# Another order for the second part of a hand-ordered attention and gated-convolution kernel

## The chip, the cores and the metric

The kernel runs on one core of one Trainium2 chip. The metric is the device time of one execution in microseconds (us). A core has TensorE (matmuls; PE in the profile, its weight loads PEld), VectorE (DVE), ScalarE (ACT), GpSimd (POOL) and SyncE (SP), which here issues most of the transfers. Each engine works through its own queue in order and waits where an operand or a buffer isn't ready.

## The reference

Two layers follow each other. The first is attention in which a query sees the first four keys (the sinks) and the 128 keys up to itself; the second takes its output `x`, gates a projection by a convolution of five taps, and projects again.

```
scores = scale * q @ k^T                    # 4 batches, 8 heads, 768 positions, 64 wide
keep   = (pos_k < 4) | (0 <= pos_q - pos_k < 128)
a      = softmax(where(keep, scores, -1e9))
x      = concat_heads(a @ v)                # 4 x 768 x 512
gate   = sigmoid(sum_k conv_w[k] * x shifted by 4 - k)
out    = (gate * (x @ w_val)) @ w_out
```

## The kernel before

`banded` (from L193) cuts the work into 24 steps s = 0 to 23: four batches, three parts of 256 positions (p = 0, 1, 2), and two halves of the heads. Two steps of one batch and part make a pair m = 0 to 11, for which the second layer runs. The order of the work isn't found by a scheduler. `ORDER` (L36 to L81) is a string of 849 names, and the last lines of `banded` call one small function for each name under `manual_schedule`, so that every engine takes its instructions in the order of that list:

```python
with tc.manual_schedule():
    for n in ORDER.split():
        f, args = events[n]
        f(*args)
```

The names, with the step or pair behind the point, and the engine that works:

- `kq`, `vv`: loads of keys and queries, and of values (three buffers each), issued by SyncE; where p = 0, `vv` also loads the sinks' values, and `sv` (ScalarE, then GpSimd) splits them.
- `s0`, `s1` (L395 to L411): scores of one half of the step, 64 TensorE matmuls that use the array in tiles of 64 by 32, then masking and the maximum on VectorE. `e0`, `e1` (L413): the exponentials on ScalarE. `rec`, `norm`: the reciprocal and the products on GpSimd.
- `tx` (L448): 16 transposes of the weights on TensorE, tiles of 64 by 128. `px` (VectorE) and `py` (ScalarE) copy them out. `sk` (L461): one transpose of the sinks' weights, full array; `ts` copies it out, on ScalarE for steps under 6 and on VectorE from there on.
- `vl` (L500): weights by values, 48 matmuls (32 where p = 0), tiles of 64 by 64, into the one buffer `xv`. `si` (L517): two matmuls more for the sinks, tiles of 64 by 128, which end the same sums.
- `xc`, `xh`, `hd` (ScalarE) read `xv`; `xl` (GpSimd) makes the low half of x; `c4` (GpSimd) and `c0`, `c1` (VectorE, eight operations) are the convolution; `c0` and `c1` read `xv` too. `th` is the gate (ScalarE).
- `v0` to `v3` (L567): x by `w_val`, twelve matmuls each, full array, the last four with the low half. `g0`, `g1` (VectorE), `h0`, `h1` (ScalarE), `l0`, `l1` (GpSimd): the gated product and its two halves gh and gl.
- `o0` to `o3` (L607): by `w_out`, six matmuls each, full array (twelve of half the width for the last block). `t0`, `t1` (ScalarE) copy the sums out, `d0`, `d1` (SyncE) send them.

The PSUM memory that TensorE writes is shared out by two small rotations: `pairs`, two buffers that serve `s0`, `s1`, `tx` and at the end `o`, and `homes`, two that serve `sk`, `v` and `o`. A buffer is taken again when its last reader is done (`e0` or `e1` for scores, `px` and `py` for `tx`, `ts` for `sk`, `g` for `v`, `t` for `o`). `tx` of a step waits for its `norm`, `vl` for `px` and `py` and for the convolution of the step before.

Of the kernel before, what the change touches and what calls it, by code (L numbers as in the profile page):

```python
# [51 lines left out]
h1.2 c1.6 e1.9 rec.9 l1.2 o3.2 e1.10 d1.0 t1.2 tx.8 xl.6 px.8 py.8 vl.7 si.7 xc.7 hd.7 xh.7 sk.8 norm.9 ts.8
c4.7 s0.10 tx.9 th.6 px.9 c0.7 d1.11 c1.7 o1.2 t0.2 e0.10 rec.10 xl.7 v0.3 vv.8 py.9 v1.3 vv.9 g0.3 h0.3 kq.12
s0.12 kq.11 s0.11 th.7 d1.2 l0.3 vl.8 si.8 xc.8 hd.8 c4.8 xh.8 d0.2 s1.11 sk.9 e0.11 norm.10 ts.9 xl.8 v2.3
e1.11 v3.3 c0.8 c1.8 g1.3 e0.12 h1.3 o2.3 s1.12 l1.3 kq.13 s1.13 rec.11 e1.12 rec.12 vl.9 si.9 xc.9 th.8 c4.9
hd.9 xh.9 tx.10 px.10 kq.16 py.10 o3.3 t1.3 vv.10 norm.11 o0.3 o1.3 t0.3 c0.9 c1.9 sk.10 ts.10 s0.13 tx.11
py.11 px.11 norm.12 xl.9 vv.13 vl.10 si.10 xc.10 hd.10 xh.10 kq.14 d1.3 tx.12 py.12 px.12 c4.10 c0.10 warm_up
v0.4 xl.10 v1.4 g0.4 d1.1 h0.4 l0.4 vv.11 c1.10 th.9 v2.4 e1.13 v3.4 g1.4 sk.11 ts.11 s1.14 s0.14 h1.4 vl.11
si.11 o0.4 sk.12 ts.12 e0.13 rec.13 l1.4 xc.11 hd.11 c4.11 sv.13 e0.14 norm.13 c0.11 o1.4 kq.18 e1.14 t0.4
c1.11 kq.15 o2.4 d0.3 o3.4 s0.18 s0.15 vv.12 th.11 xh.11 sv.12 vl.12 si.12 t1.4 xc.12 tx.13 rec.14 hd.12 xl.11  # L60
v0.5 c4.12 norm.14 xh.12 e0.15 px.13 c0.12 c1.12 v2.5 xl.12 v3.5 g1.5 py.13 th.10 v1.5 g0.5 h0.5 sk.13 ts.13
s1.15 h1.5 s1.18 d0.4 e1.15 vl.13 l0.5 si.13 o0.5 l1.5 xc.13 rec.15 hd.13 xh.13 s0.16 e0.16 th.12 tx.14 px.14
o2.5 kq.17 o1.5 t0.5 py.14 c4.13 c0.13 o3.5 t1.5 vv.14 e0.18 xl.13 vv.18 c1.13 s1.16 d1.5 sk.14 ts.14 norm.15
sk.15 ts.15 sv.18 vl.14 si.14 xc.14 hd.14 tx.15 px.15 e1.16 c4.14 c0.14 rec.16 py.15 norm.16 e1.18 c1.14 xh.14
v0.6 v1.6 g0.6 v2.6 h0.6 s0.17 vv.15 kq.19 s0.19 vl.15 si.15 rec.18 l0.6 th.13 vv.16 e0.17 xc.15 v3.6 g1.6
xl.14 c4.15 s1.17 hd.15 s1.19 th.14 h1.6 sk.16 ts.16 l1.6 xh.15 c0.15 xl.15 e1.17 rec.17 kq.20 e0.19 o0.6 o1.6
# [825 lines left out]
```

## Time and profile before

| | us |
|---|---|
| median of 3 runs | 263.9 |
| lowest and highest of the 3 | 263.66, 264.38 |
| the profiled execution's own time | 264.63 |
| its span, first to last instruction | 262.8 |
| TensorE busy | 253.6 |
| VectorE busy | 204.7 |
| ScalarE busy | 188.7 |
| GpSimd busy | 177.4 |

The profile is of one execution. Its engines' times are those in which an instruction was at work; the time of the execution holds the span and 1.8 us around it. Matmuls overlap, so the duration of one is longer than the distance to the next, and their ends are modelled; starts are recorded.

### The profile page before, as it was taken

Reading aid. Unit: us, or ns where it says so; the run is one execution under the profiler, and the core shown is the slowest. Engines: PE = TensorE matmul, PEld = TensorE weight load, DVE = VectorE, ACT = ScalarE, POOL = GpSimd, SP = SyncE. Lnnn points to the kernel's source line nnn. Section 1 sums busy time; section 2 is a strip of 40 time slices with the busy share of each in tenths; the row PEclk is TensorE's granted clock in tenths of the full one; section 3 lists DMA queues with packets and bytes.
Section 4 is the critical chain, followed back from the end, with each engine's and each line's share of the span. In section 5 each row is a group of like instructions: output and inputs, shape, how many; then the busy total and the mean of one; then the engine's idle time right before and its main releaser. Section 6 shows DMA issues by size and latency. Waiting matters only on the chain.

```text
span 262.8 us, 9921 instructions
## 1 busy us (share of the span) xinstructions
PE 253.6 (97%) x3960; PEld 205.5 (78%) x3964; DVE 204.7 (78%) x561; ACT 188.7 (72%) x692; POOL 177.4 (67%) x241
## 2 busy tenths in 40 slices
PE   7899989999999999999999999999999999999993
PEld 2355569779878878889879779889779788888982
DVE  5976999979979879997869698796878659667610
ACT  3899998979887677974796688986676768444231
POOL 6279897778668992878379665894782985933340
PEclk9999999999999999999999999999999999999998
DMA  6999382364323534755250529253407131030013
GB/s 201 379 340 341 113 262 74 109 168 144 106 78 118 183 131 146 218 171 180 63 174 2 161 81 326 78 185 111 142 4 231 68 106 59 2 122 0 2 44 128
DMA packets 27541, 36.45 MB, mean 139 GB/s; under 512 B 2272, under 2 KB 24032, under 8 KB 27488
## 3 DMA queue, kind: packets, MB, share of 16 engines
q1 hardware_dynamic: 26672, 34.96, 41.7%
q10 hardware_dynamic: 816, 0.79, 0.9%
q8 instruction: 33, 0.54, 0.9%
q14 instruction: 20, 0.16, 0.2%
HBM read 29.45 MB, written 6.29 MB: 136 GB/s over the span
## 4 chain that ended last, share of the span: by engine, by line
PE 79%; ACT 9%; POOL 4%; DMA 4%; DVE 1%; issue 1%; POOLq 0%
PE ac L576 24%; PE ac L629 22%; PE xv L513 11%; PE pr L395 9%; PE pr L455 4%; ACT w L420 4%; PE pr L629 3%; PE xv L521 2%; DMA raw<-in_w_val_dram 2%; DMA vs<-in_vsk_dram 2%; POOL xl L544 1%; PE ac L463 1%; POOL gl L605 1%; POOL vh L263 1%; ACT wv_p L140 1%
## 5 line engine op out<-in xcount | busy, mean ns | idle before, releaser
L557 DVE SCALAR_TENSOR_TENSOR sg<-xv,cw,sg 128x256 f32<-128x256 f32 x192 | 77.8, 474 | 3.3 <-POOL sg L549 2.9
L435 POOL TENSOR_TENSOR wx<-w,sm 128x512 f32<-128x512 f32 x48 | 49.2, 1047 | 5.7 <-DVE sm L427 4.0
L420 ACT ACTIVATE w<-pr,ngm 128x132 f32<-128x132 f32 x136 | 48.6, 370 | 1.6
L576 PE MATMUL ac<-xh,wvh 128*128 128x256 f32 x192 | 48.7, 288 | 0.0
L605 POOL TENSOR_TENSOR gl<-sg,gh 128x512 fp32r<-128x512 f32 x24 | 30.8, 1290 | 26.0 <-ACT gh L601 25.8
L576 PE MATMUL ac<-xh,wvl 128*128 128x256 f32 x192 | 47.0, 279 | 0.0
L549 POOL TENSOR_TENSOR sg<-xt,cw 128x512 f32<-128x512 f32 x24 | 25.5, 1063 | 17.9 <-ACT xt L528 16.5
L576 PEld LDWEIGHTS ac<-xh,wvh 128*128 128x128 f32 x192 | 36.2, 189 | 1.7 <-issue 0.5
L576 PEld LDWEIGHTS ac<-xh,wvl 128*128 128x128 f32 x192 | 36.1, 188 | 0.2
L395 PE MATMUL pr<-k,q 64*32 64x168 f32 x1536 | 35.0, 307 | 0.6 <-DVE wt L486 0.2
L513 PEld LDWEIGHTS xv<-wt,v 64*64 64x64 f32 x1024 | 30.3, 133 | 6.1 <-issue 2.6
L513 PE MATMUL xv<-wt,v 64*64 64x192 f32 (+2 forms) x1024 | 34.5, 278 | 0.2 <-ACT wt L494 0.2
L544 POOL TENSOR_TENSOR xl<-xt,xh 128x512 fp32r<-128x512 f32 x24 | 31.0, 1290 | 3.9 <-DVE sm L427 2.5
L629 PE MATMUL ac<-woh,gh 128*128 128x512 f32 x80 | 33.2, 415 | 0.0
L629 PE MATMUL ac<-woh,gl 128*128 128x512 f32 x80 | 31.8, 397 | 0.3 <-POOL gl L605 0.3
L629 PE MATMUL ac<-wol,gh 128*128 128x512 f32 x80 | 31.7, 396 | 0.0
L576 PE MATMUL ac<-xl,wvh 128*128 128x256 f32 x192 | 30.4, 280 | 0.1
L395 PEld LDWEIGHTS pr<-k,q 64*32 64x32 f32 x1536 | 24.0, 106 | 8.1 <-issue 2.1
L400 DVE COPY_PREDICATED pr<-low,pr 128x256 f32<-128x256 uint8 x48 | 20.3, 422 | 9.6 <-PE pr L395 4.9
L420 ACT ACTIVATION_READ_ACCUMULATOR w<-pr,ngm 128x1 f32 x136 | 27.6, 203 | 0.0
L576 PEld LDWEIGHTS ac<-xl,wvh 128*128 128x128 f32 x192 | 25.9, 188 | 0.3 <-POOL xl L544 0.3
L404 DVE TENSOR_REDUCE ngm<-pr 128x4 f32<-128x528 f32 x34 | 24.0, 707 | 1.2
(156 smaller groups left out, 480.0 us busy)
## 6 DMA issues: line engine op xcount, KB each, us to landing
k<-in_kt_dram SPq DMA_DIRECT2D x23, 408.0 KB, 4.1
v<-in_vt_dram SPq DMA_DIRECT2D x16, 384.0 KB, 3.9
q<-in_qt_dram SPq DMA_DIRECT2D x23, 256.0 KB, 4.6
out_dram<-osb SPq DMA_DIRECT2D x23, 256.0 KB, 2.5
v<-in_vt_dram SPq DMA_DIRECT2D x8, 256.0 KB, 5.0
raw<-in_w_out_dram SPq DMA_DIRECT2D x4, 512.0 KB, 6.6
raw<-in_w_val_dram SPq DMA_DIRECT2D x3, 512.0 KB, 6.3
raw<-in_w_val_dram ACTq DMA_DIRECT2D x1, 512.0 KB, 5.2
```

The source lines that it names most:

```text
L395: nc.tensor.matmul(ss[e * QB:(e + 1) * QB, j, c * n + x0:c * n + x1], q[js, g, (4 * c + e) * QB:(4 * c + e + 1) * QB], k[js, g, (2 * c + e ...
L400: nc.vector.copy_predicated(sv[:, :, :, :D], low[:, None, None, :].to_broadcast([P, 2, 2, D]), sv[:, :, :, 2 * HB:])
L404: nc.vector.tensor_reduce(out=ngm[:, g], in_=sv[:, :, :, :PK], axis=mybir.AxisListType.X, op=ALU.max)
L420: nc.scalar.activation(out=w[:, g, j, c], in_=sx[:, j, c, :PK], func=AF.Exp, scale=0.125 if whole else -1.0, bias=ngm[:, g, j, c:c + 1], a ...
L435: nc.gpsimd.tensor_tensor(out=t[:, n].rearrange("p c h x -> p h c x"), in0=w[:, :, :, at], in1=sm.to_broadcast([P, 4, 2, D]), op=ALU.mult)
L513: nc.tensor.matmul(acc[o * D:(o + 1) * D, g, x0 + h * D:x0 + (h + a1 - a0 + 1) * D], v[js, g, n], t[js, n % 2, n // 2, g, a0:a1 + 1].rearr ...
L544: nc.gpsimd.tensor_tensor(out=half(xls, s, "xl", F32R), in0=xts[s], in1=half(xhs, s, "xh", F32R).bitcast(F32), op=ALU.subtract)
L549: nc.gpsimd.tensor_tensor(out=half(sg, s, "sg", F32), in0=xts[s], op=ALU.mult, in1=cw[:, g, KT - 1:].to_broadcast([P, 2, PQ]))
L557: nc.vector.scalar_tensor_tensor(out=g, in0=x, scalar=a, in1=g, op0=ALU.mult, op1=ALU.add)
L576: nc.tensor.matmul(acc[:, h], a[:, kc, cs], x[:, kc], start=(n == 0), stop=(n == 11))
L605: nc.gpsimd.tensor_tensor(out=gl, in0=g, in1=gh.bitcast(F32), op=ALU.subtract)
L629: nc.tensor.matmul(acc, a[:, kc, ts], x[:, kc], start=(kc + n == 0), stop=(kc + n == 5))
```

## The change

The first 218 names of `ORDER` stay, which ends with `vv.4`, shortly ahead of the scores of step 7. The other 631 names are the same names in another order. Nothing else changes. Cut to the lines that the text speaks of:

```diff
@@ -45,39 +45,39 @@
-s0.7 l0.1 vl.4 y1.1 g1.1 e0.7 h1.1 l1.1 s1.7 s1.8 o2.1 si.4 e1.7 tx.5 xc.4 xh.4 px.5 hd.4 c4.4 c0.4 c1.4 o3.1
-t1.1 o0.1 e1.8 py.5 kq.9 sk.5 ts.5 norm.6 o1.1 t0.1 tx.6 py.6 rec.7 vl.5 si.5 xc.5 xl.4 px.6 c4.5 sk.6 ts.6
-hd.5 xh.5 xl.5 s0.9 s0.8 th.4 norm.7 v0.2 v1.2 e0.9 c0.5 tx.7 c1.5 e0.8 rec.8 norm.8 v2.2 py.7 px.7 g0.2 h0.2
...
-l1.7 vl.17 si.17 xc.17 c4.17 hd.17 xh.17 e0.21 xl.17 norm.20 d1.6 c0.17 tx.19 py.19 o2.7 o3.7 o1.7 t0.7 c1.17
-th.17 px.19 t1.7 kq.23 d1.7 s1.21 vl.18 d0.7 si.18 xc.18 c4.18 hd.18 vv.19 xh.18 e1.21 sv.19 tx.20 vv.20 px.20
...
-rec.21 s0.22 xc.19 hd.19 l0.8 xh.19 c4.19 xl.19 sk.20 o0.8 ts.20 o1.8 c0.19 c1.19 norm.21 e1.22 t0.8 d0.8 o2.8
...
-v2.10 v1.10 th.22 g0.10 v3.10 h0.10 l0.10 vl.23 si.23 xc.23 c4.23 hd.23 xh.23 xl.23 th.21 flag g1.10 o0.10
...
-o1.10 l1.11 o1.11 t0.10 d0.10 t0.11 o3.10 t1.10 o2.11 d1.10 d0.11 o3.11 t1.11
+y1.1 s1.7 s0.7 g1.1 vl.4 si.4 l0.1 tx.5 xc.4 xh.4 h1.1 c4.4 d1.0 hd.4 px.5 c0.4 c1.4 s1.8 vv.7 l1.1 sk.5 o2.1
+ts.5 norm.6 py.5 e0.7 e1.7 o0.1 o1.1 xl.4 rec.7 t0.1 vl.5 kq.10 tx.6 si.5 e1.8 py.6 xh.5 sk.6 warm_up norm.7
+o3.1 xc.5 ts.6 px.6 th.4 kq.9 xl.5 s0.8 t1.1 hd.5 e0.8 s0.9 c4.5 v0.2 c0.5 v1.2 sv.7 kq.12 g0.2 v2.2 rec.8
...
+ts.9 c0.8 c1.8 vv.9 v3.3 l0.3 d0.1 o2.3 g1.3 e0.11 e1.11 s1.13 th.8 norm.10 h1.3 xl.8 s0.13 rec.11 vl.9 l1.3
...
+c0.11 o1.4 vv.19 d0.3 c1.11 e1.14 norm.13 xh.11 tx.13 t1.4 d1.11 t0.4 px.13 xl.11 vl.12 si.12 s1.15 py.13
+xc.12 kq.19 hd.12 s0.15 v0.5 sv.13 th.10 th.11 xh.12 sk.13 c4.12 kq.16 vv.15 ts.13 rec.14 v1.5 c0.12 c1.12
...
+s0.16 sk.14 l1.5 xc.13 d0.4 c4.13 o0.5 xl.12 vv.14 ts.14 o1.5 c0.13 xl.13 e0.16 o2.5 c1.13 py.14 norm.15 s1.19
+s1.16 vl.14 tx.15 e1.18 t0.5 si.14 hd.14 xc.14 px.15 c4.14 o3.5 v0.6 t1.5 sk.15 e1.16 py.15 c0.14 ts.15 th.13
...
+tx.16 sk.16 v3.6 ts.16 hd.15 g1.6 py.16 xl.15 kq.20 v0.7 v1.7 d1.5 px.16 c4.15 e1.17 rec.17 c0.15 c1.15 sv.19
+v2.7 s0.19 s0.20 h0.6 e1.19 vl.16 h1.6 g0.7 norm.17 tx.17 si.16 kq.21 e0.19 rec.19 th.15 v3.7 l1.6 l0.6 px.17
+xc.16 hd.16 g1.7 o0.6 c4.16 sk.17 e0.20 c0.16 vv.18 s0.21 ts.17 py.17 vv.17 norm.19 h1.7 xh.16 s1.20 o1.6
...
+d0.5 sk.19 px.18 l0.7 xc.17 o0.7 kq.23 ts.19 sk.18 c4.17 py.19 xh.17 norm.20 ts.18 hd.17 o1.7 c0.17 px.19 o2.7
...
+xc.19 s0.22 sk.20 ts.20 c4.19 o0.8 hd.19 vv.20 th.18 xh.19 l1.8 xl.19 e1.22 norm.21 e0.22 c0.19 o1.8 v2.9
...
+l0.11 o0.11 flag l1.11 d1.9 o1.11 t0.10 o3.10 t0.11 d0.10 t1.10 d1.10 o2.11 d0.11 o3.11 t1.11
```

On TensorE this makes two lists of 196 operations. Operations of one kind that stand next to each other form a group. Sorted by whether the groups ahead and behind use the array in the same tiles (s 64 by 32, vl 64 by 64, tx and si 64 by 128, the others the full array):

| group | neighbours | before | after |
|---|---|---|---|
| sk | both in other tiles (scores behind) | 2 and one double | 1 |
| sk | other ahead, full array behind | 6 | 11 |
| sk | full array ahead, other behind | 7 | 1 |
| sk | full array on both sides | 2 | 6 |
| tx | both in other tiles | 8 | 3 and one double |
| tx | behind si | 7 and two doubles | 3 |
| tx | ahead of si | 0 | 9 and one double |
| si | no tx beside it | 11 | 7 |
| si | ahead of tx | 9 | 3 |
| si | behind tx | 0 | 10 |
| scores | two in a row | 13 | 14 |
| scores | one alone | 8 | 6 |
| v or o | behind a group in other tiles | 21 | 14 |
| v or o | ahead of a group in other tiles | 19 | 23 |
| all | changes of tiles from group to group | 98 | 89 |

## Rows read from the trace of the kernel before

**Rows 1.** Busy time by stretch: PE, PEld, DVE, ACT, POOL (instructions), clock, DMA share.

```profile
110.00:120.00 10.00, 10.00 (x225) 8.16 (x206) 9.42 (x41) 7.30 (x27) 7.66 (x11) 1.00 0.61 187
```

**Rows 2.** TensorE's weight loads in order of time: start, duration, what, idle time before.

```profile
80.57 0.30 PEld L576 LDWEIGHTS ac<-xl,wvh 128*128 128x128 f32 x2 [0.34 <-POOL xl L544]
```

**Rows 3.** TensorE's matmuls in order of time around 206 us, merged by form.

```profile
205.17 0.39 PE L521 MATMUL xv<-skt,vh 64*128 64x256 f32 x2
205.66 1.38 PE L395 MATMUL pr<-k,q 64*32 64x168 f32 x64
206.96 0.33 PE L463 MATMUL ac<-ident,skb 128*128 128x128 f32 x1
207.04 0.48 PE L629 MATMUL ac<-woh,gh 128*128 128x512 f32 x1
...
208.04 0.50 PE L629 MATMUL ac<-woh,gl 128*128 128x512 f32 x1 [0.28 <-POOL gl L605]
```

**Rows 4.** ScalarE in order of time around 200 us.

```profile
197.73 0.60 ACT L528 ACTIVATE xt<-xv 128x512 f32<-128x512 f32 x1 [0.59 <-PE xv L521]
...
202.72 0.31 ACT L260 ACTIVATE vh<-vs 128x128 fp32r<-128x128 f32 x1 [1.91 <-DMA vs<-in_vsk_dram]
```

**Rows 5.** TensorE's matmuls in order of time around 130 us.

```profile
127.14 0.27 PE L463 MATMUL ac<-ident,skb 128*128 128x128 f32 x1
127.34 1.37 PE L395 MATMUL pr<-k,q 64*32 64x168 f32 x64
...
130.12 0.38 PE L521 MATMUL xv<-skt,vh 64*128 64x256 f32 x2
130.43 0.50 PE L629 MATMUL ac<-woh,gh 128*128 128x512 f32 x1
...
131.94 0.27 PE L463 MATMUL ac<-ident,skb 128*128 128x128 f32 x1
131.97 0.47 PE L629 MATMUL ac<-woh,gh 128*128 128x512 f32 x1
```

**Rows 6.** TensorE's matmuls in order of time around 96 us.

```profile
95.63 0.80 PE L395 MATMUL pr<-k,q 64*32 64x168 f32 x32
96.36 0.71 PE L455 MATMUL pr<-ident,wx 64*128 64x64 f32 x16
97.01 0.50 PE L629 MATMUL ac<-woh,gh 128*128 128x512 f32 x1
```

**Rows 7.** TensorE's matmuls in order of time around 197 us.

```profile
197.30 0.39 PE L521 MATMUL xv<-skt,vh 64*128 64x256 f32 x2
197.53 0.66 PE L455 MATMUL pr<-ident,wx 64*128 64x64 f32 x16
198.11 0.38 PE L576 MATMUL ac<-xh,wvh 128*128 128x256 f32 x1
```

**Rows 8.** TensorE's matmuls in order of time around 46 us.

```profile
46.31 0.71 PE L455 MATMUL pr<-ident,wx 64*128 64x64 f32 x16
46.83 0.36 PE L521 MATMUL xv<-skt,vh 64*128 64x256 f32 x2
47.12 0.80 PE L395 MATMUL pr<-k,q 64*32 64x168 f32 x32
```

**Rows 9.** The chain that ended last, from 23 to 26 us.

```profile
24.07 1.52 ACT w L420 x8
```

**Rows 10.** VectorE in order of time, from 84 to 126 us.

```profile
89.86 3.22 DVE L557 SCALAR_TENSOR_TENSOR sg<-xv,cw,sg 128x256 f32<-128x256 f32 x8
...
110.66 0.43 DVE L400 COPY_PREDICATED pr<-low,pr 128x256 f32<-128x256 uint8 x1
...
111.99 0.42 DVE L400 COPY_PREDICATED pr<-low,pr 128x256 f32<-128x256 uint8 x1
```

**Rows 11.** The page's costliest groups: busy us, mean ns, idle before.

```profile
L549 POOL TENSOR_TENSOR sg<-xt,cw 128x512 f32<-128x512 f32 x24 | 25.5, 1063 | 17.9 <-ACT xt L528 16.5
```

**Rows 12.** The page's DMA issues: size of one, median us to landing.

```profile
v<-in_vt_dram SPq DMA_DIRECT2D x8, 256.0 KB, 5.0
```

More of the change, by code (lines that the diff above doesn't have):

```diff
@@ L47 @@
 e1.5 kq.8 c0.3 scalars d0.0 py.4 rec.5 v0.1 v1.1 y0.1 c1.3 e1.6 rec.6 v2.1 norm.5 g0.1 th.3 h0.1 v3.1 vv.4
-s0.7 l0.1 vl.4 y1.1 g1.1 e0.7 h1.1 l1.1 s1.7 s1.8 o2.1 si.4 e1.7 tx.5 xc.4 xh.4 px.5 hd.4 c4.4 c0.4 c1.4 o3.1
-t1.1 o0.1 e1.8 py.5 kq.9 sk.5 ts.5 norm.6 o1.1 t0.1 tx.6 py.6 rec.7 vl.5 si.5 xc.5 xl.4 px.6 c4.5 sk.6 ts.6
-hd.5 xh.5 xl.5 s0.9 s0.8 th.4 norm.7 v0.2 v1.2 e0.9 c0.5 tx.7 c1.5 e0.8 rec.8 norm.8 v2.2 py.7 px.7 g0.2 h0.2
-s1.9 kq.10 s1.10 vl.6 l0.2 si.6 xc.6 c4.6 th.5 sk.7 ts.7 hd.6 d0.1 vv.7 v3.2 xh.6 sv.7 o2.2 g1.2 c0.6 o0.2
@@ L52 @@
[L52 to L66, printed above, removed]
@@ L67 @@
-t0.6 tx.16 py.16 c1.15 px.16 v0.7 v1.7 norm.18 sk.18 ts.18 s0.20 d1.4 kq.21 e1.19 d0.6 vl.16 v2.7 e0.20 g0.7
-h0.7 norm.17 l0.7 si.16 xc.16 c4.16 hd.16 tx.18 px.18 py.18 tx.17 v3.7 px.17 c0.16 o2.6 o3.6 th.15 g1.7 vv.23
-rec.19 xh.16 c1.16 py.17 t1.6 s1.20 h1.7 xl.16 s0.21 e1.20 sk.17 ts.17 norm.19 o0.7 vv.17 th.16 rec.20 d0.5
-l1.7 vl.17 si.17 xc.17 c4.17 hd.17 xh.17 e0.21 xl.17 norm.20 d1.6 c0.17 tx.19 py.19 o2.7 o3.7 o1.7 t0.7 c1.17
-th.17 px.19 t1.7 kq.23 d1.7 s1.21 vl.18 d0.7 si.18 xc.18 c4.18 hd.18 vv.19 xh.18 e1.21 sv.19 tx.20 vv.20 px.20
@@ L72 @@
-c0.18 v2.8 xl.18 v3.8 g1.8 h1.8 kq.22 c1.18 th.18 v0.8 v1.8 sk.19 py.20 ts.19 g0.8 h0.8 vl.19 si.19 s1.22 l1.8
-rec.21 s0.22 xc.19 hd.19 l0.8 xh.19 c4.19 xl.19 sk.20 o0.8 ts.20 o1.8 c0.19 c1.19 norm.21 e1.22 t0.8 d0.8 o2.8
-e0.22 rec.22 v0.9 norm.22 th.19 tx.21 px.21 py.21 vl.20 si.20 vv.21 xc.20 c4.20 hd.20 xh.20 xl.20 s1.23 e1.23
-s0.23 vv.22 v1.9 g0.9 h0.9 o3.8 t1.8 v2.9 e0.23 v3.9 l0.9 c0.20 c1.20 rec.23 sk.21 norm.23 ts.21 vl.21 si.21
-xc.21 c4.21 g1.9 h1.9 l1.9 tx.22 py.22 px.22 tx.23 py.23 hd.21 xh.21 o2.9 xl.21 o0.9 o3.9 c0.21 o1.9 t1.9 t0.9
@@ L77 @@
-c1.21 px.23 th.20 sk.22 ts.22 vl.22 si.22 xc.22 c4.22 xh.22 xl.22 sk.23 ts.23 d1.9 hd.22 c0.22 c1.22 v0.10
-v2.10 v1.10 th.22 g0.10 v3.10 h0.10 l0.10 vl.23 si.23 xc.23 c4.23 hd.23 xh.23 xl.23 th.21 flag g1.10 o0.10
-o2.10 d1.8 c0.23 c1.23 v0.11 v1.11 th.23 g0.11 h0.11 l0.11 v2.11 d0.9 v3.11 g1.11 o0.11 h1.10 l1.10 h1.11
-o1.10 l1.11 o1.11 t0.10 d0.10 t0.11 o3.10 t1.10 o2.11 d1.10 d0.11 o3.11 t1.11
+y1.1 s1.7 s0.7 g1.1 vl.4 si.4 l0.1 tx.5 xc.4 xh.4 h1.1 c4.4 d1.0 hd.4 px.5 c0.4 c1.4 s1.8 vv.7 l1.1 sk.5 o2.1
@@ new lines @@
+ts.5 norm.6 py.5 e0.7 e1.7 o0.1 o1.1 xl.4 rec.7 t0.1 vl.5 kq.10 tx.6 si.5 e1.8 py.6 xh.5 sk.6 warm_up norm.7
+o3.1 xc.5 ts.6 px.6 th.4 kq.9 xl.5 s0.8 t1.1 hd.5 e0.8 s0.9 c4.5 v0.2 c0.5 v1.2 sv.7 kq.12 g0.2 v2.2 rec.8
+e0.9 d1.1 sk.7 v3.2 c1.5 tx.7 th.5 vl.6 norm.8 ts.7 py.7 si.6 h0.2 vv.12 g1.2 xc.6 l0.2 vv.8 px.7 s1.10 h1.2
+hd.6 xh.6 s1.9 c4.6 e1.10 c0.6 o0.2 c1.6 o2.2 e1.9 rec.9 s0.12 l1.2 o3.2 xl.6 s1.12 vl.7 t1.2 tx.8 si.7 xc.7
+hd.7 xh.7 kq.11 norm.9 px.8 c4.7 xl.7 py.8 e0.12 e1.12 sk.8 ts.8 s0.10 e0.10 o1.2 kq.13 c0.7 c1.7 th.6 v0.3
@@ new lines @@
+v1.3 t0.2 tx.9 vl.8 px.9 py.9 g0.3 rec.10 si.8 th.7 xc.8 d0.2 s0.11 s1.11 v2.3 xh.8 h0.3 c4.8 sk.9 vv.10 hd.8
+ts.9 c0.8 c1.8 vv.9 v3.3 l0.3 d0.1 o2.3 g1.3 e0.11 e1.11 s1.13 th.8 norm.10 h1.3 xl.8 s0.13 rec.11 vl.9 l1.3
+kq.14 si.9 kq.18 tx.10 xc.9 sk.10 hd.9 ts.10 px.10 xh.9 o3.3 o0.3 e0.13 c4.9 c0.9 c1.9 o1.3 s1.18 norm.11
+py.10 sv.12 s0.14 kq.17 vl.10 xl.9 t0.3 tx.11 si.10 sk.11 rec.12 t1.3 v0.4 e1.13 py.11 xc.10 c4.10 hd.10 ts.11
+v1.4 xh.10 px.11 c0.10 c1.10 vv.11 e0.14 v2.4 g0.4 d1.2 v3.4 norm.12 th.9 g1.4 s0.18 d1.3 s1.14 h0.4 vl.11
@@ new lines @@
+tx.12 h1.4 si.11 vv.13 l0.4 rec.13 py.12 l1.4 sk.12 kq.15 ts.12 o0.4 xc.11 xl.10 o2.4 c4.11 px.12 o3.4 hd.11
+c0.11 o1.4 vv.19 d0.3 c1.11 e1.14 norm.13 xh.11 tx.13 t1.4 d1.11 t0.4 px.13 xl.11 vl.12 si.12 s1.15 py.13
+xc.12 kq.19 hd.12 s0.15 v0.5 sv.13 th.10 th.11 xh.12 sk.13 c4.12 kq.16 vv.15 ts.13 rec.14 v1.5 c0.12 c1.12
+norm.14 v2.5 v3.5 vl.13 g0.5 e0.18 g1.5 e1.15 tx.14 si.13 px.14 e0.15 h0.5 h1.5 rec.15 th.12 hd.13 l0.5 xh.13
+s0.16 sk.14 l1.5 xc.13 d0.4 c4.13 o0.5 xl.12 vv.14 ts.14 o1.5 c0.13 xl.13 e0.16 o2.5 c1.13 py.14 norm.15 s1.19
@@ new lines @@
+s1.16 vl.14 tx.15 e1.18 t0.5 si.14 hd.14 xc.14 px.15 c4.14 o3.5 v0.6 t1.5 sk.15 e1.16 py.15 c0.14 ts.15 th.13
+c1.14 v1.6 vv.16 rec.16 s0.17 rec.18 g0.6 norm.16 s1.17 th.14 v2.6 xh.14 e0.17 vl.15 xl.14 si.15 xc.15 xh.15
+tx.16 sk.16 v3.6 ts.16 hd.15 g1.6 py.16 xl.15 kq.20 v0.7 v1.7 d1.5 px.16 c4.15 e1.17 rec.17 c0.15 c1.15 sv.19
+v2.7 s0.19 s0.20 h0.6 e1.19 vl.16 h1.6 g0.7 norm.17 tx.17 si.16 kq.21 e0.19 rec.19 th.15 v3.7 l1.6 l0.6 px.17
+xc.16 hd.16 g1.7 o0.6 c4.16 sk.17 e0.20 c0.16 vv.18 s0.21 ts.17 py.17 vv.17 norm.19 h1.7 xh.16 s1.20 o1.6
@@ new lines @@
+sv.18 e0.21 o2.6 norm.18 l1.7 e1.20 c1.16 o3.6 d1.4 th.16 vl.17 tx.19 vv.21 rec.20 t1.6 h0.7 t0.6 tx.18 si.17
+d0.5 sk.19 px.18 l0.7 xc.17 o0.7 kq.23 ts.19 sk.18 c4.17 py.19 xh.17 norm.20 ts.18 hd.17 o1.7 c0.17 px.19 o2.7
+d1.6 py.18 o3.7 c1.17 s1.21 vl.18 xl.16 xl.17 t1.7 tx.20 si.18 t0.7 v2.8 px.20 hd.18 xc.18 v0.8 v1.8 vv.23
+c4.18 xh.18 c0.18 e1.21 py.20 th.17 c1.18 xl.18 g0.8 kq.22 rec.21 v3.8 g1.8 vl.19 si.19 h0.8 s1.22 l0.8 h1.8
+xc.19 s0.22 sk.20 ts.20 c4.19 o0.8 hd.19 vv.20 th.18 xh.19 l1.8 xl.19 e1.22 norm.21 e0.22 c0.19 o1.8 v2.9
@@ new lines @@
+c1.19 rec.22 s1.23 th.19 s0.23 d0.6 v3.9 vl.20 t0.8 e1.23 e0.23 vv.22 tx.21 si.20 v0.9 g1.9 xc.20 v1.9 norm.22
+d1.7 rec.23 hd.20 px.21 h1.9 xh.20 o2.8 c4.20 g0.9 c0.20 sk.21 c1.20 h0.9 o3.8 tx.22 ts.21 py.21 norm.23 l0.9
+tx.23 vl.21 t1.8 si.21 l1.9 sk.22 ts.22 py.22 xl.20 xc.21 o0.9 c4.21 d1.8 py.23 px.22 hd.21 o2.9 xh.21 d0.8
+c0.21 th.20 o1.9 o3.9 t0.9 c1.21 vl.22 si.22 t1.9 sk.23 xc.22 xh.22 xl.21 ts.23 v0.10 px.23 v2.10 c4.22 v1.10
+hd.22 c0.22 v3.10 th.21 c1.22 g0.10 h0.10 g1.10 vl.23 xl.22 l0.10 si.23 xc.23 hd.23 o0.10 c4.23 xh.23 c0.23
@@ L81 @@
+o2.10 xl.23 v0.11 h1.10 v1.11 c1.23 th.22 v2.11 v3.11 g0.11 th.23 g1.11 l1.10 h0.11 o1.10 h1.11 d0.7 d0.9
+l0.11 o0.11 flag l1.11 d1.9 o1.11 t0.10 o3.10 t0.11 d0.10 t1.10 d1.10 o2.11 d0.11 o3.11 t1.11
 """
```

## The prediction

> **What bounds the kernel now.** I read the busy time by stretches first. In the ten microseconds from 110 us TensorE is busy for all ten at the full granted clock, VectorE for 9.42, ScalarE for 7.30 and GpSimd for 7.66 [rows 1]; in the other stretches between 40 and 200 us TensorE is full in the same way, or within 0.13 us of it. The end is therefore set by the sum of TensorE's queue, and a new order can change two things only: how much time TensorE loses inside that queue, and what it waits for. "Busy" hides both, because the ends of matmuls are modelled. So I read TensorE's timeline by starts: the time of a group is from its first start to the first start of the next group.
>
> Waits that hide there, from the scores of step 7 on: TensorE's weight loads for v0.2 wait 0.34 us for xl.5 [rows 2]. The sinks' product si.19 takes 0.49 us to the next start, where si.11 takes 0.31 [rows 3, 5]: 0.18. The first two matmuls of o0.8 take 1.00 us, because the third waits for gl [rows 3]; all six of o0.4 take 1.51 [rows 5], so that two of them need no more than 0.6, and at least 0.4 is lost. The last two have one source: the sink values of step 19 are late, ScalarE stands 1.91 us for their transfer at 202.72 [rows 4], and what follows on ScalarE and GpSimd is late with it. In all 0.34 + 0.18 + 0.4 = 0.9 us.
>
> What neighbours cost. From step 7 on the list gives TensorE 196 operations. I sorted them by the shape in which they use the array: full (sk, v, o), 64 by 128 (tx, si), 64 by 64 (vl), 64 by 32 (scores). A group costs more where its neighbour has another shape:
> - sk: 0.20 between v and scores, 0.03 between two o [rows 5], 0.08 between scores and o [rows 3].
> - tx: 0.65 with other shapes on both sides [rows 6], 0.58 behind si [rows 7], 0.52 ahead of si [rows 8].
> - si: 0.31 between other shapes [rows 5], 0.23 ahead of tx [rows 7], 0.29 behind tx [rows 8].
> - scores: 0.73 alone [rows 6], 1.30 for two in a row [rows 3].
>
> **The change, part by part.** The same instructions run, so nothing is added or taken away; I take the counts of neighbours (the table in the section on the change) and price them with these rows.
> 1. sk. Before: 2 x 0.03 + 6 x 0.08 + 9 x 0.20, and one pair at 0.08 + 0.20, in all 2.6. After: 6 x 0.03 + 11 x 0.08 + 2 x 0.20 = 1.5. Gain 1.1; the two or three that stand between si and scores are priced like those between v and scores.
> 2. tx. Before: 8 x 0.65 + 7 x 0.58 and two doubles behind si at 0.58 + 0.50: 11.4 (0.50 is what sixteen transposes add, about the 0.52 ahead of si). After: 3 x 0.65 + 9 x 0.52 + 3 x 0.58 and doubles at 1.15 and 1.02: 10.5. Gain 0.9. The 0.52 comes from one place; were it 0.58, the gain would be 0.3.
> 3. si. Before: 11 x 0.31 + 9 x 0.23 = 5.5. After: 7 x 0.31 + 3 x 0.23 + 10 x 0.29 = 5.8. Loss 0.3.
> 4. scores. 13 pairs and 8 single groups become 14 and 6: one pair more at 1.30, two singles fewer at 0.73. Gain 0.2.
> 5. v and o. Groups of these that follow another shape fall from 21 to 14, those that another shape follows rise from 19 to 23. At the smallest difference above, 0.09 for each, that is 3 x 0.09 = 0.3 gained; the cuts between sk, v and o, which become more by some eight at up to 0.03, give 0.2 back. I take 0.1; the bounds are nothing and 0.3.
>
> The sum is 1.1 + 0.9 - 0.3 + 0.2 + 0.1 = 2.0 us less on TensorE; with the doubtful 0.52 at its other end 1.4, with step 5 at its upper end 2.2.
>
> 6. The waits that go. Between si.5 and v0.2 stand sk.6 and two scores; the new list adds o3.1, six matmuls and so some 1.5 us [rows 5], more than the 0.34 that xl.5 is late. The load of step 19 leaves its place in SyncE's queue behind two output sends of pair 7 for one behind vl.11, some 70 us ahead of its use, so its transfer no longer holds ScalarE. Gain 0.9, and nothing is late next at these two places.
>
> 7. The waits that may come. For each TensorE operation I held the queue of the engine that frees it against the TensorE work in between. The closest place is s0.21, which needs the PSUM pair of s0.20, so the exponentials e0.20. From the end of s0.19 TensorE has s0.20 (1.30 - 0.73 = 0.57), vl.16 (1.48, as vl.11: 130.12 less 127.34, less 1.30 for the scores between), tx.17, si.16, v3.7 and o0.6 (twelve and six matmuls, 1.5 each), and sk.17: 0.57 + 1.48 + 0.52 + 0.29 + 3.0 + 0.20 = 6.1 us [rows 3, 5, 8]. In that time VectorE masks s0.19, 1.33 [rows 10], and ScalarE does e0.19, 1.52 [rows 9], rec.19, th.15, xc.16 (0.60 for each of the two long ones) [rows 4], hd.16 and e0.20: 1.33 + 1.52 + 0.2 + 0.6 + 0.6 + 0.2 + 1.7 = 6.2, and 0.1 for a handoff: 0.2 late. Two other places (vl.14 behind the convolutions of step 13, o0.7 behind its low half) come out within 0.1 of zero. The bounds are 0, where engines run a little ahead, and the 0.9 us that the old list loses in its own close places; I take 0.3, since only one place comes out late.
>
> 8. Loads. SyncE's queue is in order, so each load also stands behind the sends and loads ahead of it. With that, the shortest room from issue to use is now that of vv.9, vv.14 and kq.16, 6.0 to 6.8 us; the slowest kind of step load lands in 5.0 us [rows 12]. They are covered by about a microsecond, and I price them at nothing; if the cover goes, it is the first rival.
>
> Sum: -2.0 - 0.9 + 0.3 = -2.6 us. The profiled execution took 264.63 us, 1.8 above its span and 0.7 above the median of the three runs; the terms are differences, and I carry them to the median: 263.9 - 2.6 = **261.3 us**.
>
> In the Trainium skill, TensorEngine Tiling (Array Packing), Tiling Modes, it says that a change of the tiling mode, not of the tile, drains TensorE; TensorE: Matmul & The Clock Gate, Step-by-step, has the drain at some 128 cycles. At 2.4 GHz that is 53 ns, as an estimate, and the nine changes of shape that go would by these pages give 0.5 us in place of 2.0, so 262.8 us in all.
>
> **The rivals.**
> - *A load becomes the wait* (chance 0.10). Three loads have some 6 us of room. If they land two microseconds later than the 5.0 of [rows 12], each holds TensorE by about 0.8, together 2.4: 261.3 + 2.4 = 263.7 us, no change. For it: the small transfer of sink values held ScalarE for 1.91 us [rows 4]. Against: it alone of the step loads after 40 us did so.
> - *Only the number of shape changes counts* (0.10), which falls from 98 to 89, each at the smallest difference that rows show, si at 0.31 against 0.23 [rows 5, 7]: 9 x 0.09 = 0.8 in place of 2.0, so 262.5 us, still faster. Against: sk costs 0.03 or 0.20 by its neighbours [rows 5], more than one price. The rule of the Trainium skill above is of this kind.
> - *The convolutions become the bound* (0.06), the case that ends slower. There is one PSUM buffer for values: vl of a step can't start until the convolutions of the step before have read it. The chain from si is xc 0.60 [rows 4], c4 1.06 [rows 11], eight VectorE operations 3.22 [rows 10] and four handoffs of about 0.1: 5.3 us. The new list puts tx ahead of si ten times, which takes its work out of that loop; the shortest loop, si.4 to vl.5, holds tx.5, one scores, sk.5 and 18 matmuls of o, 5.8 us. VectorE is busy for 9.42 of 10 in [rows 1], so it may enter the loop late. It decides once VectorE is more than 0.5 us late in every loop: 0.25 more than that in each of 20 steps is 5 us, so 261.3 + 5 = 266.3 us. Against: the old list has a loop as short (si.17 to vl.18: tx.19, 18 matmuls of o and one scores, 5.7), and TensorE doesn't wait there.
> - *The order doesn't do what it says*: the engines would have to leave the list. The old list stands in the trace operation by operation, and I give this no chance of its own.
>
> **How the numbers follow.** The forecast has 0.74. A difference under 0.3% (0.8 us) can't be told from no change here, so faster means under 263.1. Faster: 0.74 + 0.10, less 0.02 for more close places than I saw, 0.82; within: 0.10 and 0.01 of these; slower: 0.06 and the other 0.01. So 0.82, 0.11, 0.07. The range: step 5 at its upper end, sk between si and scores and o0.8's wait each 0.1 to 0.2 better, and no new wait give some 3.4, 260.5; at the top it takes in the shape rival and the lower ends of steps 2 and 7 (1.4 + 0.9 - 0.9 = 1.4 gained, 262.5) and goes to 263.1, short of the load rival and of the convolutions.
>
> **What would show it.** Right: sk mostly at 0.03 to 0.08 from start to start, tx ahead of si at 0.52, scores in 20 groups, no ScalarE wait for sink values, and the last matmul some 2.6 us earlier. Wrong: tx ahead of si at 0.6 or more (step 2), gaps of over 0.5 us inside or ahead of TensorE's groups at s0.21, vl.9 or vl.14 (steps 7 and 8), or VectorE without idle time from one si to the next vl (the third rival).

## The result, and the profile after

The kernel after takes 261.81 us (median of 6 runs, 261.48 to 262.49) against 263.94 of the kernel before on the same chip: a ratio of 0.9914, 95% interval 0.9902 to 0.9926, so 2.1 us less. A second measurement, among the experiments, gave 0.9936 (0.9918 to 0.9954). The forecast was 261.3 with a range of 260.5 to 263.1, and 0.82 on faster.

The profiled execution took 261.48 us with a span of 259.7. The first scores of step 7 and the last matmul in it, then the same two of the kernel before:

```profile
64.16 1.37 PE L395 MATMUL pr<-k,q 64*32 64x168 f32 x64
...
255.28 0.27 PE L625 MATMUL ac<-woh,gl 128*128 128x256 f32 x1
```

```profile
64.58 0.80 PE L395 MATMUL pr<-k,q 64*32 64x168 f32 x32
...
257.98 0.27 PE L625 MATMUL ac<-woh,gl 128*128 128x256 f32 x1
```

From start to start that is 191.1 us after and 193.4 before: 2.3 of the 3.1 by which the spans differ lie in the stretch that the change orders; the rest lies ahead of it and behind it. The medians differ by 2.1, since the profiled execution of before was 0.7 above its median and that of after 0.3 below. All sums below are over this stretch, with 0.12 for the last matmul (191.24 and 193.52).

TensorE is as full as before, and VectorE (9.62 of 10) a little fuller, in the stretch of [rows 1]:

```profile
110.00:120.00 10.00, 10.00 (x231) 8.04 (x221) 9.62 (x42) 7.38 (x27) 8.79 (x13) 1.00 0.74 245
```

**The waits that went.** TensorE around si.19 and o0.8, as in [rows 3]:

```profile
202.92 0.39 PE L521 MATMUL xv<-skt,vh 64*128 64x256 f32 x2
203.23 1.37 PE L395 MATMUL pr<-k,q 64*32 64x168 f32 x64
204.53 0.33 PE L463 MATMUL ac<-ident,skb 128*128 128x128 f32 x1
204.62 0.48 PE L629 MATMUL ac<-woh,gh 128*128 128x512 f32 x1
...
205.18 0.40 PE L629 MATMUL ac<-woh,gl 128*128 128x512 f32 x1
```

si.19 takes 0.31 to the next start (0.49 before), the first two matmuls of o0.8 0.56 (1.00 before). ScalarE's copy of the sink values of step 19 and the weight load with the low half in v0.2 stand for nothing now (no idle time is given behind them), where [rows 4] and [rows 2] had 1.91 and 0.34:

```profile
169.46 0.29 ACT L260 ACTIVATE vh<-vs 128x128 fp32r<-128x128 f32 x1
```

```profile
79.24 0.54 PEld L576 LDWEIGHTS ac<-xl,wvh 128*128 128x128 f32 x4
```

**The neighbours.** TensorE in order of time from the end of o1.1, the new pattern at its plainest: o, vl.5, tx.6 ahead of si.5, sk.6, o3.1.

```profile
72.50 0.40 PE L629 MATMUL ac<-wol,gh 128*128 128x512 f32 x1
72.73 0.40 PE L629 MATMUL ac<-woh,gl 128*128 128x512 f32 x1
73.06 1.55 PE L513 MATMUL xv<-wt,v 64*64 64x64 f32 x48
74.54 0.71 PE L455 MATMUL pr<-ident,wx 64*128 64x64 f32 x16
75.06 0.36 PE L521 MATMUL xv<-skt,vh 64*128 64x256 f32 x2
75.36 0.33 PE L463 MATMUL ac<-ident,skb 128*128 128x128 f32 x1
75.44 0.48 PE L629 MATMUL ac<-woh,gh 128*128 128x512 f32 x1
75.75 0.39 PE L629 MATMUL ac<-wol,gh 128*128 128x512 f32 x1
75.99 0.39 PE L629 MATMUL ac<-woh,gl 128*128 128x512 f32 x1
```

tx ahead of si takes 0.52, si behind tx 0.30, sk behind si 0.08: the prices of the prediction. But two intervals are ones that it hadn't priced. A change of shape can cost on both its sides: I call the time lost on the last matmul ahead of it the exit, and that lost on the first one or two behind it the entry. The last matmul of o ahead of vl takes 0.33 where one inside o takes 0.23, an exit of 0.10, and the first o behind sk takes 0.31, 0.08 too much. Compare an o behind scores, with sk at the other end, around s0.21:

```profile
178.34 0.39 PE L629 MATMUL ac<-woh,gl 128*128 128x512 f32 x1
178.57 0.27 PE L463 MATMUL ac<-ident,skb 128*128 128x128 f32 x1
178.77 1.37 PE L395 MATMUL pr<-k,q 64*32 64x168 f32 x64
180.07 0.50 PE L629 MATMUL ac<-woh,gh 128*128 128x512 f32 x1
180.41 0.40 PE L629 MATMUL ac<-wol,gh 128*128 128x512 f32 x1
```

Behind scores the first o takes 0.34, hardly more than behind sk. So an sk at the head of the full-array work is cheap, and the operation behind it still pays most of the entry. The two scores, 32 matmuls each, take 1.30, so s0.21, the place that step 7 had 0.2 late, is on time.

Summed by operation over the stretch, from start to next start (us):

| | before | after | difference | step of the prediction |
|---|---|---|---|---|
| sk | 2.86 | 1.54 | -1.32 | -1.1 |
| tx | 11.41 | 10.70 | -0.71 | -0.9 |
| si | 5.67 | 5.81 | +0.14 (+0.31 without si.19's wait) | +0.3 |
| scores | 22.77 | 22.67 | -0.10 | -0.2 |
| v and o, the last o included | 123.27 | 122.95 | -0.32 (two waits of 0.95 went) | -0.1 |
| vl | 27.56 | 27.57 | 0 | 0 |

In the line of v and o the waits that went (0.40 at v0.2, 0.55 at o0.8) should have given 0.95; only 0.32 came, so v and o cost some 0.6 more elsewhere. Not all of it is neighbours. Some groups of after take longer than groups with the same neighbours do in the other traces: tx.5 by 0.11 (67.16 to 67.86, where tx between si and another shape else takes 0.59), the scores of step 11 by 0.06 (1.36 for 1.30), and four groups of v and o, o3.3 among them, by 0.04 each; 0.3 in all. Without these 0.3 and the 1.1 of waits that went, the neighbours gave 1.32 at sk, 0.8 at tx and 0.16 at the scores, and cost 0.3 at si and some 0.5 at v and o: 1.5 us less for nine changes of shape less, 0.17 each.

### The profile page after: what moved, and what is told of

It is laid out like the page before. It is cut to its first block, busy times and chain, and to the rows that moved or that the text cites. A ratio compares the mean times of both kernels' runs of the same rounds, so it can differ in the third digit from the quotient of the medians.

```text
span 259.7 us, 9934 instructions
## 1 busy us (share of the span) xinstructions
PE 252.4 (97%) x3960; PEld 204.9 (79%) x3964; DVE 204.2 (79%) x561; ACT 187.0 (72%) x692; POOL 177.2 (68%) x241
## 4 chain that ended last, share of the span: by engine, by line
PE 84%; ACT 9%; DMA 2%; POOL 2%; DVE 1%; issue 1%
PE ac L576 27%; PE ac L629 22%; PE xv L513 12%; PE pr L395 10%; PE pr L455 5%; ACT w L420 4%; PE pr L629 3%; PE xv L521 2%; DMA raw<-in_w_val_dram 2%; PE ac L463 2%; ACT wv_p L140 1%; ACT wv_p L159 1%; ACT wvl L186 1%; PE ac L625 1%; PE pr L625 1%
```

## The experiments

**A. One load earlier in the kernel before.**

```diff
-th.17 px.19 t1.7 kq.23 d1.7 s1.21 vl.18 d0.7 si.18 xc.18 c4.18 hd.18 vv.19 xh.18
+th.17 px.19 t1.7 kq.23 vv.19 d1.7 s1.21 vl.18 d0.7 si.18 xc.18 c4.18 hd.18 xh.18
```

> The kernel before with one step moved: the load of values and sink values of step 19 is issued ahead of the two output sends of pair 7, so that ScalarE no longer stands for it; TensorE's list keeps every neighbour. Theory (the new order gains about 1.6 us by fewer changes of shape and some 0.7 to 1.0 us by waits that go, 0.6 of them from this load): 0.6 us less than before, 263.3 us; si.19 takes 0.31 us instead of 0.49 to the next start, the first two matmuls of o0.8 take 0.6 or less instead of 1.00. Rival 1 (the whole gain of the new order is waits that go): about 2 us less, 261.9. Rival 2 (something else is late at these places as well, so the wait only changes its name): no difference, 263.9.

Measured: 263.47 us beside 264.11, ratio 0.9967 (0.9955 to 0.998), 0.6 less; the stretch 192.82 instead of 193.52. TensorE around si.19 and o0.8:

```profile
204.92 0.39 PE L521 MATMUL xv<-skt,vh 64*128 64x256 f32 x2
205.24 1.37 PE L395 MATMUL pr<-k,q 64*32 64x168 f32 x64
206.54 0.33 PE L463 MATMUL ac<-ident,skb 128*128 128x128 f32 x1
206.62 0.47 PE L629 MATMUL ac<-woh,gh 128*128 128x512 f32 x1
...
207.17 0.40 PE L629 MATMUL ac<-woh,gl 128*128 128x512 f32 x1
```

si.19 takes 0.32, the first two of o0.8 0.55, and the group v0.2, v1.2 is as late as before. That one load was worth 0.7 of the stretch's 2.3, so the gain isn't all in waits, and the two places had one cause, as the prediction says.

**B. si ahead of tx in the ten places.** TensorE's list at one of them:

```diff
-vl.10 tx.11 si.10 sk.11
+vl.10 si.10 tx.11 sk.11
...
```

> The kernel after with si ahead of tx instead of behind it in the ten places where the new order has them together; the number of changes of shape stays 89. Theory (what counts is that the two stand together, and a change of shape is paid once, whoever comes first): tx 0.58 instead of 0.52, si 0.23 instead of 0.29, no difference beyond 0.1 us, 261.8. Rival (tx gains only where it stands ahead of si, by the 0.58 against 0.52 of the rows): 0.6 us more, 262.4.

Measured: 261.92, ratio 0.9907 (0.9889 to 0.9926); the stretch 191.11 against 191.24 of after. It doesn't matter which comes first. The lower price of tx ahead of si, which the prediction had from one place, is real, but si pays it back: the tx of the stretch together take 0.66 more, the si 0.68 less.

**C. Six pairs parted.** The TensorE list at the first of them:

```diff
-vl.5 tx.6 si.5 sk.6 o3.1
+vl.5 si.5 sk.6 tx.6 o3.1
...
```

> The kernel after with six of the ten pairs of tx and si parted: tx goes behind the next TensorE operation after si, and the two copies of its result with it. This makes 11 changes of shape more (100 instead of 89) and, by the queues laid end to end, no wait over 0.1 us more. Theory (a change of shape costs 0.16 us, exit and entry together): 1.8 us more than after, 263.6. Rival 1 (0.09 us for each, the smallest difference of the rows, as the second rival of the prediction has it): 1.0 more, 262.8. Rival 2 (53 ns for each, the estimate worked out from the Trainium skill, TensorE: Matmul & The Clock Gate, Step-by-step): 0.6 more, 262.4. Rival 3 (the gain of the new order is waits, and shapes cost nothing): no difference, 261.8.

Measured: 263.88, ratio 0.9997 (0.9982 to 1.0013), 2.0 more than B beside it; the stretch 193.21, 1.97 more than after. TensorE at the first parted pair:

```profile
74.47 0.38 PE L521 MATMUL xv<-skt,vh 64*128 64x256 f32 x2
74.78 0.33 PE L463 MATMUL ac<-ident,skb 128*128 128x128 f32 x1
75.04 0.71 PE L455 MATMUL pr<-ident,wx 64*128 64x64 f32 x16
75.68 0.50 PE L629 MATMUL ac<-woh,gh 128*128 128x512 f32 x1
76.02 0.40 PE L629 MATMUL ac<-wol,gh 128*128 128x512 f32 x1
```

From si to the second o it is 0.31 + 0.26 + 0.64 + 0.34 = 1.55; in after tx, si, sk and the first o take 0.52 + 0.30 + 0.08 + 0.31 = 1.21. That is 0.34 for two changes more, 0.17 each. Of the 1.97, 0.25 lies at two places whose neighbours stay the same (o3.3, see H, and sk.18), so 11 changes cost 1.7, 0.16 each. The prices of 0.09 and of 53 ns are too low, and that shapes cost nothing is out.

**D. Three sk elsewhere in the same surroundings.** TensorE's list at the first:

```diff
-v0.2 v1.2 v2.2 sk.7 v3.2 tx.7
+v0.2 v1.2 v2.2 v3.2 sk.7 tx.7
...
```

> The kernel after with three sk moved inside their surroundings of v and o, or to the other edge of them, so that another shape follows: sk.7 from between v2.2 and v3.2 to behind v3.2, sk.15 from between v0.6 and v1.6 to behind v1.6, sk.23 from behind si.22 to ahead of vl.22. The number of changes of shape stays 89. By the prices of the prediction's step 1 (0.03 between v or o, 0.08 behind another shape, 0.20 ahead of one): 0.17 + 0.17 + 0.12 = 0.46 us more than after, 262.3. Theory (an sk is one more full-array operation; its cheap 0.03 or 0.08 is paid back by the v or o behind it, and where it costs 0.20 it takes the exit from the operation ahead): 0.05 more, 261.9; a v ahead of the moved sk takes 0.09 less than ahead of another shape, and the v behind its old place 0.08 less than behind sk.

Measured: 262.04, ratio 0.9918 (0.9897 to 0.9938); the runs can't tell 0.46 from 0.05, but the starts can. First after, then D:

```profile
82.63 0.27 PE L463 MATMUL ac<-ident,skb 128*128 128x128 f32 x1
82.65 0.37 PE L576 MATMUL ac<-xh,wvh 128*128 128x256 f32 x1
82.86 0.28 PE L576 MATMUL ac<-xh,wvl 128*128 128x256 f32 x1
...
83.68 0.63 PE L576 MATMUL ac<-xl,wvh 128*128 128x256 f32 x4
84.23 0.71 PE L455 MATMUL pr<-ident,wx 64*128 64x64 f32 x16
```

```profile
83.51 0.63 PE L576 MATMUL ac<-xl,wvh 128*128 128x256 f32 x4
83.98 0.27 PE L463 MATMUL ac<-ident,skb 128*128 128x128 f32 x1
84.19 0.71 PE L455 MATMUL pr<-ident,wx 64*128 64x64 f32 x16
```

sk goes from 0.02 to 0.21. But the last four of v3.2, which end at tx in the first case and at sk in the second, go from 0.55 to 0.47, and the v behind sk, which took 0.21, takes 0.12 behind a v. Over the stretch (191.43) the sk took 0.47 more (2.01 instead of 1.54), as the prediction's prices have it; v took 0.32 less (58.36 instead of 58.68), and the group of o0.9, which now ends at sk.23, 0.13 less. What is left, 0.20, is again o3.3 (4.62 instead of 4.42). Where an sk stands beside v and o costs nothing that can be measured, as long as the number of changes is the same.

**E. After once more.**

> The kernel after, unchanged, on the same chip as the runs beside it, so that they are read against it: 261.8 us, 2.1 less than before.

Measured: 262.33 beside 264.23, 0.9936 (0.9918 to 0.9954); the stretch 191.50, 0.26 more than in the first profile of after, 0.18 of it in the group of o3.3 and 0.09 in that of o0.9.

**F. VectorE made later.**

```diff
                 nc.vector.scalar_tensor_tensor(out=g, in0=x, scalar=a, in1=g, op0=ALU.mult, op1=ALU.add)
+        if s >= 6 and taps[-1] == KT - 2:
+            g = sg[s // 2][:, 2 * steps[s][2]:2 * steps[s][2] + 2]
+            nc.vector.tensor_scalar(out=g, in0=g, scalar1=1.0, scalar2=None, op0=ALU.mult)
```

> The kernel after with one more VectorE operation in the convolution of steps 6 to 23: sg is multiplied by 1.0 in place behind the last tap, so that VectorE is later by that operation's time in each loop from si to the next vl; TensorE's list is the same. The nearest row, a one-input VectorE operation of half the elements, takes 0.42 us; I expect 0.35 to 0.5. Theory (VectorE has 0.2 to 0.5 us of room in most loops, and the new order lost nothing there): queues laid end to end give 1.3 us more than after at 0.35 and 2.7 more at 0.5, so 263.1 to 264.5; the waits come ahead of vl. Rival 1 (the third rival of the prediction, VectorE without room in every loop): 18 times the operation, 6 to 9 us more, 268 to 271. Rival 2 (VectorE is idle for 3 to 4 us in 20, so it is hidden): no difference, 261.8.

Measured: 264.79, ratio 1.0021 (1.0007 to 1.0034), 2.5 more than E. The groups of VectorE by form have the added operation (busy us, mean ns | idle before); the second fence has the longest new wait on TensorE:

```profile
L560 DVE TENSOR_SCALAR sg<-sg 128x512 f32<-128x512 f32 x18 | 10.3, 570 | 0.6
```

```profile
121.73 0.71 PE L455 MATMUL pr<-ident,wx 64*128 64x64 f32 x16 [0.77 <-DVE ngm L409]
```

VectorE does 10.3 us more and the kernel gets 2.5 longer: three quarters of it fell into room that was there. The longest wait comes at tx.11 and not ahead of vl, as I had expected of most. (tx.11 takes the PSUM pair of s1.18. In a step with p = 0 VectorE's last masking operation, L409, is the last to read the scores there, and not e0 or e1.) The third rival, no room anywhere, would have been 10.3. (Why the mean is 0.57 stands in the last section.)

**G. A third and a fourth order**, found from the prices of changes and a queue by queue account. What mattered in the third, against after, at step 21:

```diff
-o0.9 c4.21 d1.8 py.23 px.22 hd.21 o2.9 xh.21 d0.8 c0.21 th.20 o1.9 o3.9 t0.9 c1.21 vl.22
+o2.9 d1.8 py.22 o0.9 o1.9 o3.9 c4.21 xl.20 py.23 hd.21 d0.8 t0.9 px.22 xh.21 c0.21 c1.21 vl.22
...
```

> A third order of the same operations from the scores of step 7 on, found from the measured prices: 86 changes of shape instead of 89, one pair of scores more, and no place where an engine is late if VectorE takes 0.2 us more in each step. Theory (0.16 us for each change, the pair worth 0.16, and the 0.14 us of waits left in after): 0.8 us less than after, 261.0. Rival 1 (0.09 for each change): 0.3 + 0.1 less, 261.4. Rival 2 (with fewer changes something else comes late): no difference or slower than 261.8.

> A fourth order, with 86 changes of shape as well and 0.02 us less on TensorE by the prices, but with less room in the convolutions' loops: if VectorE takes 0.2 us more in each step, six places come late by 0.8 us together. Theory: 0.8 us less than after where the queues run as laid out, 261.0, and up to 0.8 more than that where they don't; so the same as the third order or slower. Rival (room doesn't matter, the sum of TensorE alone sets the time): the same as the third order within 0.1.

Measured: 276.49 (ratio 1.0486, 1.0457 to 1.0514) and 268.52 (1.0173, 1.0153 to 1.0193). Both expectations failed, and the one that the order with less room would be the slower too. In the third order the groups take some 15 us more than groups with the same neighbours do in the other traces; 12.1 of it are ten waits of TensorE, so the run says nothing on the price of a change. (The fourth order loses about 3 there, and 4 more behind the last matmul, where ScalarE waits 3.4 us for an output buffer.) The costliest wait of the third, on ScalarE, VectorE and TensorE, and the stretch that starts 0.9 us after TensorE goes on:

```profile
234.48 0.60 ACT L648 ACTIVATE osb<-ac 128x512 f32<-128x512 f32 x1 [3.66 <-PE ac L629]
```

```profile
236.02 3.22 DVE L557 SCALAR_TENSOR_TENSOR sg<-xv,cw,sg 128x256 f32<-128x256 f32 x8 [4.13 <-ACT xh L536]
```

```profile
239.50 0.73 PE L513 MATMUL xv<-wt,v 64*64 64x64 f32 x20 [3.66 <-DVE sg L557]
```

```profile
240.40:243.70 3.30, 3.30 (x34) 2.96 (x27) 1.17 (x3) 1.54 (x4) 0.83 (x1) 0.50 0.03 5
```

In this stretch, behind the stand of 3.66 us, the granted clock is 0.50, the lower of its two levels (1.2 instead of 2.4 GHz), and TensorE is busy throughout; at half speed it can lose up to 1.7 us more in it (an estimate, half of the 3.3 us). So a wait of TensorE can cost more than its own length.

t0.9 stands ahead of xh.21 on ScalarE and waits for the last of o1.9. The convolution waits for xh.21, and vl.22 for the convolution. My account had the convolution wait for hd.21 alone. So one step of ScalarE was moved:

```diff
-t0.9 px.22 xh.21 c0.21
+px.22 xh.21 t0.9 c0.21
```

> The third order (276.5 us) with one step of ScalarE's queue moved: the output copy t0.9, which waits for the last matmul of o1.9, goes behind the copy xh.21 instead of ahead of it; TensorE's list is the same. In the run of the third order ScalarE stands 3.66 us for that matmul, VectorE's convolution of step 21 waits 4.13 us for xh.21, and TensorE loses 3.7 us at vl.22. Theory (the third order lost its time in a queue: one copy in front of the convolution's release): about 3.5 us less, 273, and vl.22 no longer late by more than 0.3 us. Rival (the convolution is late for another reason, the sends or the low halves): no difference, 276.5.

Measured: 273.53 (four runs from 271.33 to 275.30; ratio 1.0335, 1.0263 to 1.0408), 3.0 less, and the two intervals don't meet. ScalarE, then VectorE:

```profile
232.20 0.60 ACT L536 ACTIVATE xh<-xv 128x512 fp32r<-128x512 f32 x1
235.83 0.60 ACT L648 ACTIVATE osb<-ac 128x512 f32<-128x512 f32 x1 [3.03 <-PE ac L629]
```

```profile
233.25 3.23 DVE L557 SCALAR_TENSOR_TENSOR sg<-xv,cw,sg 128x256 f32<-128x256 f32 x8
```

The copy now waits behind xh.21, and the wait at vl.22 is gone. The next one is longer: vl.23 waits 2.07 us for the convolution, where it waited 1.29 in the third order. The clock at 0.50 comes at other places in this profile (70.5 to 73.8 and 248.0 to 251.3, both behind a stand of TensorE), so the difference of the two runs holds some of that too. Whether the convolution would have started at hd.21, without xh.21, wasn't tried; nor were its other gaps, or those of the fourth order, taken apart.

**H. Two edits to after.**

```diff
-s1.9 c4.6 e1.10 c0.6 o0.2 c1.6 o2.2 e1.9 rec.9 s0.12 l1.2 o3.2 xl.6 s1.12 vl.7
+s1.9 c4.6 e1.10 c0.6 o0.2 c1.6 o2.2 e1.9 rec.9 l1.2 o3.2 xl.6 s0.12 s1.12 vl.7
...
-h1.3 xl.8 s0.13 rec.11 vl.9 l1.3
+h1.3 l1.3 xl.8 s0.13 rec.11 vl.9
```

> The kernel after with two edits that leave the queues of VectorE, ScalarE and SyncE as they are: s0.12 moves on TensorE behind o3.2, next to s1.12, so that o2.2 and o3.2 stand together (87 changes of shape instead of 89, one pair of scores more), and on GpSimd the low half l1.3 goes ahead of xl.8, so that o3.3 doesn't wait for gl. Theory (0.17 us for a change, and a wait only where a queue is late): 0.36 less on TensorE and 0.1 to 0.25 less at o3.3, in all 0.5 us less than after, a ratio to before of 0.990 where after has 0.991 to 0.994; the group of o3.3 takes 4.4 us instead of 4.5 to 4.6. Rival 1 (0.09 for a change): 0.2 + 0.2. Rival 2 (something in the order that is not in the queues decides, as in the third and fourth order): slower than after.

Measured: 261.65 beside 263.96, ratio 0.9907 (0.9886 to 0.9928): within the interval of after. The stretch takes 191.30, after 191.24 and 191.50. The 0.36 came (from the start of o0.2 to that of vl.7 it is 5.70 instead of 6.05), and was taken back, 0.18 ahead of s0.10 and 0.22 in the group of o3.3. TensorE's weight loads at these two, and GpSimd's gl ahead of o3.3:

```profile
95.73 0.33 PEld L395 LDWEIGHTS pr<-k,q 64*32 64x32 f32 x24 [0.30 <-DVE ngm L409]
...
113.79 0.19 PEld L629 LDWEIGHTS ac<-woh,gh 128*128 128x128 f32 x1 [0.43 <-issue]
```

```profile
111.37 1.28 POOL L605 TENSOR_TENSOR gl<-sg,gh 128x512 fp32r<-128x512 f32 x1 [1.10 <-ACT gh L601]
```

s0.10 now comes before VectorE has freed its pair. The edit on GpSimd gave little: gl now waits 1.10 us for gh and starts at 111.37 instead of 111.61, 0.07 earlier against o3.3. But the wait in o3.3 is not for gl, as I had thought: the load that stands is of gh, the one of gl ahead of it went on time (113.17, when gl was done for 0.5 us), and the trace gives no engine for the wait ("issue"). What it is stays open.

## Why the prediction was right, and where its terms were off

- *What bounds.* Right: TensorE is full before and after, and what differs is what it loses by neighbours and waits (A, C). Of the signs, sk at 0.03 to 0.08, tx ahead of si at 0.52, scores in 20 groups and no ScalarE wait for sink values came as named. That the last matmul of the profile comes 2.7 us earlier, nearly the forecast, is partly luck: 0.4 of it lies ahead of the stretch.
- *Steps 1 to 4, the prices.* They hold to 0.2 each in the table: sk -1.32 against -1.1, tx -0.71 against -0.9 (the 0.52 ahead of si is right, tx.5 was 0.11 late), si +0.31 against +0.3, scores -0.10 against -0.2.
- *Step 5* is the term that was mis-sized: v and o were given 0.1 gained and a bound of nothing; their neighbours cost some 0.5 more. It counted sk as one of them, so that a v or o behind sk should have no entry to pay. The starts give 0.31 for an o behind sk, 0.34 behind scores, 0.23 inside; and D shows the same from the other side: sk's 0.47 more came with 0.45 less in v and o. So more than a third of step 1's gain went back into v and o.
- *The second rival*, that only the number of changes counts, has the better mechanism: B and D change neighbours and not their number, and cost nothing beyond o3.3. Its price was too low, since the 0.09 (0.08 in its rows) is the exit of si alone, without the entry behind it. The change's nine fewer gave 0.17 each, C's eleven more cost 0.16 each, H's two fewer gave 0.18 each. An exit of 0.10 (73.06) and an entry of 0.08 (75.75) show it in single rows. A pair of scores in place of two alone is not to be counted on top, as G's expectation does: its 0.16 is the scores' side of the two changes that go. 98 to 89 at 0.17 are 1.5, where the prediction had 2.0 and that rival 0.8.
- In the Trainium skill, TensorEngine Tiling (Array Packing), Tiling Modes, has the rule that a change of the mode drains TensorE and a change of tile alone doesn't. The trace agrees: tx and si, of one mode, take the same together in either order (0.52 + 0.29 and 0.59 + 0.22), and parting them costs (B, C). For the price, the drain of TensorE: Matmul & The Clock Gate, Step-by-step, worked out as 53 ns (an estimate), the runs give some three times as much, and the measurement decides.
- *Step 6* had 0.9, and about 1.1 went: 0.7 by the load (A), and 0.40 at v0.2, which the group of v0.2 and v1.2 was longer than others with the same neighbours. *Step 7* had 0.3 for new waits; s0.21, which it named, wasn't late, and others were (tx.5, the scores of step 11, o3.3): 0.3 in the first profile and 0.6 in the second (E). So the size of step 7 came by luck. Together 0.6 was expected, and 0.5 to 0.8 came.
- *Step 8 and the first rival.* The loads landed soon enough (4.9 us against [rows 12]; keys took 4.7, and 4.1 before), and neither vl.9 nor vl.14 nor s0.16 was late.
- *The third rival* didn't come, but F and G show how near its kind is: one VectorE operation more in each step, 0.57 on average, costs 2.5, and a copy in the wrong place of ScalarE's queue 3.

So some -1.5 by neighbours and -0.5 to -0.8 by waits make the 2.0 (E) to 2.3 us of the stretch, and the medians give 1.9 (E) to 2.1. The forecast's -2.6 was 0.5 too much, as much as its neighbours (2.0 for 1.5); step 5 alone was 0.6 off, and step 1, 0.2 better than its sum, gave some of that back.

## What to carry to other kernels

Where TensorE is full, count the places where its list changes the way the array is used, and price one by both its sides: the exit on the last matmul ahead and the entry on the first one or two behind, since an operation that looks cheap can hand its entry on. Then check each other engine's queue before the order is used: what a saved change gives (0.16 to 0.18 us) is small beside what one step ahead of its turn takes (3 us in G). Where the closest places have no room left, fewer changes can give nothing more (H).
